# Places in SBUF of the weight buffers and split operands moved by 16-byte steps; a spare strip dropped

## The chip, the cores and the metric

The kernel runs on one core of one Trainium2 chip, in one launch. The metric is the device time of a run in microseconds (us), of which the median of three runs is given. Beside it stands one execution taken by the hardware profiler, and from that one come all the rows below.

## What is computed

Hash-bucketed attention over q, k, v (2 batches, 8 heads, 768 positions, head width 64), then a dense feed-forward layer, then four experts that are mixed by probabilities:

```python
mask = q_bucket[:, :, :, None] == k_bucket[:, :, None, :]
scores = np.where(mask, scale * np.matmul(q, k.transpose(0, 1, 3, 2)), -1e9)
x = softmax(scores) @ v                     # -> 1536 x 512
h = x @ w_in                                # 512 -> 2048
x = np.where(h > 0, h, exp(min(h, 0)) - 1) @ w_out
p = domain_probs / domain_probs.sum(-1)
for e in range(4):                          # 512 -> 1024 -> 512
    out += p[:, e:e + 1] * (np.maximum(x @ w1[e], 0) @ w2[e])
```

All of it is float32. The kernel writes an operand x as a rounded high part and a rest (`hi` + `lo`, both of type fp32r), and makes one product of three matmuls: hi by hi, hi by lo, lo by hi.

## The kernel before

**Stages.** The attention comes first (to about 260 us of the span). Its end is woven into the first layer (`l1_mm`, `emit_l2`), which goes on to about 533 us. What the change's words call the second part, the experts, fills the rest (`second`, `unit`).

**The first layer** goes over (group g, block tb of 512 tokens, tile m of 128 hidden units). `l1_parts` (lines 714 to 716) makes 12 matmuls: the stationary operand is a piece of the weight tile `wt[g, m]`, the moving operand 512 columns of `xh` or `xl`. `emit_l2` (line 768) makes 12 more per tile, with pieces of the same weight tile stationary and 512 columns of the split activations `h` moving.

**The second part** goes over eight half experts gg and three token blocks tb, 24 units in all. In a unit `a_step` computes the next unit's hidden rows in four goes of 12 matmuls (lines 968 to 970: stationary a piece of a split `w1` tile, moving 512 columns of `xh`, `xl`, `xh`). Between them stand seven `product` calls (line 1021, 12 matmuls each). There the stationary operand is 128 columns of a split operand `op`, and the moving operand 256 columns of a split `w2` tile. The products come as 24, 24, 24 and 12 matmuls in a row. The order is written out by hand in `unit`; no scheduler changes it.

**Each matmul has its own weight load** (LDWEIGHTS, the page's PEld), and the load of a matmul runs while the matmul before it streams its moving operand.

**Buffers.** A split weight tile is `[P, 4, DM]`, 8192 bytes of each partition: for the first layer w_in hi, w_in lo, w_out hi, w_out lo. Eight slots are used in turn (`GM = 8`): two in pool `wa`, one in `wm`, five in `wb` (`wpool`). `split_w` takes a slot for the first layer, `slot_tile` one for the second part (two slots for `w1` and four for `w2` in each half expert). The split operands take turns in four halves of two `far` buffers of 8192 bytes (`prep_op`, `op_n % 4`). They are written by ScalarE (hi) and VectorE or GpSimd (lo), in `split2` (lines 906, 908, 910).

**Where tiles lie.** Pools grow from the left end of a partition's memory (`const`, `xp`, `wa`, `raw`, `cv`, `wb`, `near`, `accp`, ...) or from its right end (`edge`, `raw2`, `raw3`, `wm`, `far`, ...). A pool's tile begins at a multiple of 32 bytes. Two tiles only set where the others lie: `pn` is given 64 columns though 48 are used, and `edge_t` is a strip of 96 bytes at the right end, of which `emit_probs` uses 48 as scratch. With them every operand of a matmul begins at a multiple of 64 bytes.

Of the kernel before, what the change touches and what calls it, by code (L numbers as in the profile page):

```python
# [7 lines left out]
F32 = mybir.dt.float32  # L8
F32R = mybir.dt.float32r
# [7 lines left out]
P = 128  # L17
# [18 lines left out]
def lsh_attention_moe_kernel(  # L36
# [15 lines left out]
    B, H, S, D = q.shape  # L52
    NB = proj.shape[1]
    NT, DM = out.shape
    DFF = w_in.shape[1]
    E = dprobs.shape[1]
    NJ = S // P
# [6 lines left out]
    TB = 512  # L64
# [17 lines left out]
    const = ctx.enter_context(tc.tile_pool(name="const", bufs=1))  # L82
# [2 lines left out]
    wa_p = ctx.enter_context(tc.tile_pool(name="wa", bufs=NPRE))  # L85
    raw_p = ctx.enter_context(tc.tile_pool(name="raw", bufs=1))
    cv_p = ctx.enter_context(tc.tile_pool(name="cv", bufs=1))
    edge = ctx.enter_context(tc.tile_pool(name="edge", bufs=1, side="right"))
    edge_t = edge.tile([P, 24], F32, name="edge")


    late, slots, early, ps_early, ps_late = (ExitStack() for _ in range(5))
# [75 lines left out]
    def x_tiles(c):  # L168
        if c not in xh:
            xh[c], xl[c] = (xp.tile([P, NT], F32R, tag=f"x{n}{c}", name=f"x{n}{c}") for n in "hl")  # L170
        return xh[c], xl[c]

    for c in range(NC - 1):
        x_tiles(c)
    pn = const.tile([P, 64], F32, name="pn")[:, 0:B * NJ * E].rearrange("p (t e) -> p t e", e=E)

    def emit_probs():
        sm = edge_t[:, 0:B * NJ]
        nc.vector.tensor_add(sm, dp[:, :, 0], dp[:, :, 1])
        for e in range(2, E):  # L180
            nc.vector.tensor_add(sm, sm, dp[:, :, e])
        nc.vector.tensor_scalar(out=sm, in0=sm, scalar1=1e-9, scalar2=None, op0=ALU.add)
        nc.vector.reciprocal(out=sm, in_=sm)
        nc.vector.tensor_tensor(out=pn, in0=dp, in1=sm.unsqueeze(2).to_broadcast([P, B * NJ, E]),
                                op=ALU.mult)
# [5 lines left out]
    wraw, w32, wt = {}, {}, {}  # L191
# [72 lines left out]

    def split_w(g, m, pool, eng, part=None):
        if part != 1:
            wt[g, m] = pool.tile([P, 4, DM], F32R, tag="w", name="w")
        t = wt[g, m]
        for i, s in enumerate(w32[g, m]):
            if part == 1 - i:  # L270
                continue
            hi, lo = t[:, 2 * i, :], t[:, 2 * i + 1, :]
            if i == 0:
                hi = hi.rearrange("p (c f) -> p c f", f=P)
                lo = lo.rearrange("p (c f) -> p c f", f=P)
            if "p" in eng:
                nc.gpsimd.tensor_scalar(out=hi, in0=s, scalar1=1.0, scalar2=1.0, op0=ALU.mult, op1=ALU.mult)
            else:
                nc.scalar.activation(out=hi, in_=s, func=ACTF.Copy)
            if "P" in eng:  # L280
                nc.gpsimd.tensor_tensor(out=lo, in0=s, in1=hi.bitcast(F32), op=ALU.subtract)
            else:
                nc.vector.tensor_tensor(out=lo, in0=s, in1=hi.bitcast(F32), op=ALU.subtract)
        if part != 0:
            del w32[g, m]
# [356 lines left out]
    def att_step(u):  # L642
# [36 lines left out]
        if g2 >= 1 and m <= NPRE and u < NU:  # L679
            if i == 0 and k_ == 0:  # L680
                pre[:] = conv_w(0, m, cv_p, 2) + [lambda: consumed(0, m, False)]
                pre.extend(lambda n=n: split_w(0, m, wpool(m), "pP", n) for n in range(2))
                pre.append(lambda: consumed(0, m, True))
            for _ in range(i in PRE_AT if m < NPRE else LASTN[i]):
                if pre:
                    pre.pop(0)()


    pools, acc, last_x = {}, {}, []
# [36 lines left out]
    def four(pool, i, dtype, name):  # L726
        return pools[pool].tile([P, 4, TB], dtype, tag=f"{pool}{i}", name=name)
# [53 lines left out]
    def epilogue(g, tb, i, ps):  # L781
# [6 lines left out]
        if g == G1 - 1:  # L788
            last_x.append(lambda: split2(xh[i][:, ts], xl[i][:, ts], a, "av"))
            if tb < NTB - 1:  # L790
                last_x.pop()()

    def wpool(m):
        return wa_p if m < NPRE else pools["wb" if m > NPRE else "wm"]

# [27 lines left out]
    def new_conv():  # L823

        due, (g, m) = todo.pop(0)
        steps = conv_w(g, m, pools["w32"], 2)
        conv.extend((0, f) for f in steps[:6])
        conv.extend(ends)
        conv.extend((0, f) for f in steps[6:] + [lambda: consumed(g, m, False)])
        ends[:] = [(due, lambda i=i: split_w(g, m, wpool(FT.index((g, m)) % GM), "a", i)) for i in range(2)]  # L830
        ends.append((due, lambda: consumed(g, m, True)))
        if not todo:
            conv.extend(ends)
# [31 lines left out]
    ch_n, op_n, op_b = [0], [0], []  # L865

    def slot_tile():
        k_ = slot_n[0] % GM
        slot_n[0] += 1
        return wpool(k_).tile([P, 4, DM], F32R, tag="w", name="w")  # L870

    def emit_pt():

# [29 lines left out]
    def split2(hi, lo, x, eng):  # L903

        if eng[0] == "a":
            nc.scalar.activation(out=hi, in_=x, func=ACTF.Copy)  # L906
        else:
            nc.vector.tensor_copy(hi, x)
        e = nc.gpsimd if eng[1] == "p" else nc.vector
        e.tensor_tensor(out=lo, in0=x, in1=hi.bitcast(F32), op=ALU.subtract)  # L910

    def prep_w1(gg, i):

        t = slot_tile()
        x, _ = raw2(gg, i)
        for j in range(2):
            w1_t[gg, 2 * i + j] = t[:, 2 * j], t[:, 2 * j + 1]
            hi, lo = (y.rearrange("p (c f) -> p c f", f=P) for y in w1_t[gg, 2 * i + j])
            split2(hi, lo, x[:, :, j * P:(j + 1) * P], "av")
# [3 lines left out]
    def prep_w2(gg, n):  # L923

        t = slot_tile()
        b1, b2 = raw2(gg, 0)[1], raw2(gg, 1)[1]
        b11, b12, b21, b22 = b1[:, :, 0:HD], b1[:, :, HD:DM], b2[:, :, 0:HD], b2[:, :, HD:DM]
        tmp = keep["tmp"]
        v = lambda out, a, b_: nc.vector.tensor_tensor(out=out, in0=a, in1=b_, op=ALU.subtract)
        for j, nm in enumerate(PAIRS[n]):  # L930
            hi, lo = (t[:, 2 * j + k_].rearrange("p (k d) -> p k d", k=2) for k_ in range(2))
            if nm == "T2":
                v(b11, b12, b11)
                v(tmp, b22, b11)
            if nm == "T3":
                v(b12, b22, b12)
            if nm == "T4":
                v(b21, b21, tmp)
            x = {"B11": b11, "B21": b21, "T2": tmp, "T3": b12, "T1": b11, "T4": b21, "B22": b22}[nm]
            split2(hi, lo, x, "ap" if n in (1, 2) else "av")  # L940
            t_t[gg, nm] = hi, lo
        if n == 3:
            for _ in range(2):
                raw_free.append(raw_used.pop(0))
            loads()
# [32 lines left out]
    def blocks(u):  # L978
        h = hf_t[u]
        return h[:, 0:2, 0:HT], h[:, 2:4, 0:HT], h[:, 0:2, HT:TB], h[:, 2:4, HT:TB]  # L980

    def prep_op(u, nm, eng="av"):
        a11, a12, a21, a22 = blocks(u)
        x = {"P1": a11, "P2": a12, "P3": a12, "P4": a22, "P5": keep.get("S1"), "P6": keep.get("S2"), "P7": a21}[nm]
        i = op_n[0] % 4
        op_n[0] += 1
        if i % 2 == 0 and len(op_b) < 2:
            op_b.append(four("far", i // 2, F32R, "op"))
        hi, lo = (op_b[i // 2][:, i % 2 * 2 + k_] for k_ in range(2))
        op_t[u, nm] = hi, lo  # L990
        hi, lo = (y.rearrange("p (k t) -> p k t", k=2) for y in (hi, lo))
        split2(hi, lo, x, eng)
# [55 lines left out]
    def unit(v, a, hooks):  # L1048
# [6 lines left out]

        rows(0)
        prep_op(v, "P7")
        product(v, "P1")
        nc.scalar.activation(out=keep["s1"], in_=pr_t["P1"], func=ACTF.Copy)
        product(v, "P2")  # L1060
        sums_op(v, "S4")
        prep_op(v, "P5")
        add_ps(v, "11", "P2", "s1")
        add_kept(v, "11", "s1")
        store(v, "11")
        hooks[0]()
        rows(1)
        prep_op(v, "P4")
        product(v, "P6")
        nc.vector.tensor_tensor(out=keep["u2"], in0=pr_t["P6"], in1=keep["s1"], op=ALU.add)  # L1070
# [110 lines left out]
    for u in range(NU - 2):  # L1181
        att_step(u)
        if u == PU - 2:
            emit_probs()
        if u == NU - PU - 1:
            early.close()
            for i in range(2):
                raw_free.append(open_pool(f"raw{i + 2}", 1, "right"))
            open_pool("wm", 1, "right")
            loads()  # L1190
        if u == NU - PU + 6:
            l1_start(0)
        take(parts, 1)
# [52 lines left out]
```

## Time and profile before

| | before |
|---|---|
| median of 3 runs | 1032.09 us (1031.25 to 1032.11) |
| the profiled execution: its own time | 1030.52 us |
| the profiled execution: its span | 1028.7 us |
| TensorE busy | 1008.8 us, 98% of the span |
| VectorE busy | 841.9 us, 82% |
| ScalarE busy, GpSimd busy | 521.4 us, 494.9 us |
| TensorE clock granted | full in all 40 slices |

Busy time of TensorE says that a matmul was somewhere in the array, not that the array took a column in each cycle: matmuls overlap, and their ends are modelled. So the pace is read from starts: from the start of one row of matmuls to the start of the next, over their number.

### The profile page before, as it was taken

Reading aid. Unit: us, or ns where it says so; the run is one execution under the profiler, and the core shown is the slowest. Engines: PE = TensorE matmul, PEld = TensorE weight load, DVE = VectorE, ACT = ScalarE, POOL = GpSimd, SP = SyncE. Lnnn points to the kernel's source line nnn. Section 1 sums busy time; section 2 is a strip of 40 time slices with the busy share of each in tenths; the row PEclk is TensorE's granted clock in tenths of the full one; section 3 lists DMA queues with packets and bytes.
Section 4 is the critical chain, followed back from the end, with each engine's and each line's share of the span. In section 5 each row is a group of like instructions: output and inputs, shape, how many; then the busy total and the mean of one; then the engine's idle time right before and its main releaser. Section 6 shows DMA issues by size and latency. Waiting matters only on the chain.

```text
span 1028.7 us, 16096 instructions
## 1 busy us (share of the span) xinstructions
PE 1008.8 (98%) x5886; PEld 886.5 (86%) x5886; DVE 841.9 (82%) x1292; ACT 521.4 (51%) x1024; POOL 494.9 (48%) x425
## 2 busy tenths in 40 slices
PE   8999999999999999999999999999999999999997
PEld 5898999888887888888789999999999999999996
DVE  6889888988779898624557778899899999989996
ACT  6898899898566445434523333333243233333332
POOL 3566676575356445522321243545545444454453
PEclk9999999999999999999999999999999999999999
DMA  6856566471122222100020030020200102010012
GB/s 160 186 137 161 129 168 154 111 213 58 41 83 84 81 82 82 42 1 22 5 88 1 1 103 12 1 82 8 96 11 18 65 11 93 11 49 34 1 52 72
DMA packets 72693, 72.23 MB, mean 70 GB/s; under 512 B 26132, under 2 KB 60648, under 8 KB 72616
## 3 DMA queue, kind: packets, MB, share of 16 engines
q1 hardware_dynamic: 72312, 71.14, 24.5%
q8 instruction: 47, 0.77, 0.3%
q14 instruction: 30, 0.25, 0.1%
q10 hardware_dynamic: 304, 0.07, 0.1%
HBM read 48.98 MB, written 3.21 MB: 51 GB/s over the span
## 4 chain that ended last, share of the span: by engine, by line
PE 49%; issue 6%; POOL 2%; DVE 1%; ACT 0%; DVEq 0%; POOLq 0%; ACTq 0%
PE l L1021 22%; PE r L969 4%; PE a L969 4%; PE a L968 4%; PE r L968 4%; PE r L970 4%; PE a L970 4%; POOL h L752 2%; PE l L768 1%; DVE op L910 0%; DVE a L1038 0%; DVE a L1032 0%; ACT op L906 0%; PE r L716 0%; PE r L714 0%
## 5 line engine op out<-in xcount | busy, mean ns | idle before, releaser
L1021 PEld LDWEIGHTS l<-w,op 128*128 128x128 f32 x2016 | 251.0, 188 | 8.5 <-ACT op L906 1.1
L1021 PE MATMUL l<-w,op 128*128 128x256 f32 x2016 | 253.5, 280 | 0.8 <-ACT op L906 0.6
L1038 POOL TENSOR_TENSOR a<-a,temps 128x512 f32<-128x512 f32 x62 | 94.9, 1531 | 127.1 <-DVE a L1032 127.1
L906 ACT ACTIVATE op<-hf 128x512 fp32r<-128x512 f32 x120 | 73.8, 626 | 137.3 <-DVE hf L973 84.4
L768 PE MATMUL l<-h,w 128*128 128x512 f32 x576 | 140.5, 392 | 1.1 <-ACT a L785 0.8
L910 DVE TENSOR_TENSOR op<-hf,op 128x512 fp32r<-128x512 f32 x120 | 126.8, 1070 | 5.1 <-ACT op L906 5.0
L752 POOL TENSOR_TENSOR h<-g,h 128x512 fp32r<-128x512 f32 x44 | 66.4, 1509 | 134.1 <-ACT h L748 89.1
L768 PEld LDWEIGHTS l<-h,w 128*128 128x128 f32 x576 | 107.4, 188 | 26.6 <-POOL h L752 2.2
L395 DVE TENSOR_SCALAR_CACHE_REDUCE mk<-s 128x768 f32<-128x768 f32 x96 | 91.3, 951 | 21.1 <-PE s L386 18.1
L428 DVE TENSOR_TENSOR ptl<-pt,pth 128x384 fp32r<-128x384 f32 x192 | 97.6, 550 | 11.1 <-ACT pth L431 11.1
L414 PE MATMUL pt<-cst,mk 128*128 128x128 f32 x576 | 94.9, 274 | 0.6 <-DMA rx<-d 0.4
L404 ACT ACTIVATE mk<-mk,mn 128x768 f32<-128x768 f32 x96 | 89.7, 935 | 10.8 <-DVE mk L395 10.2
L431 ACT ACTIVATE pth<-pt 128x384 fp32r<-128x384 f32 x192 | 84.0, 482 | 8.1 <-PE pt L414 7.7
L385 PE MATMUL s<-ks,qs 128*128 128x512 f32 x192 | 80.3, 441 | 7.6 <-DVE mk L395 7.2
L414 PEld LDWEIGHTS pt<-cst,mk 128*128 128x128 f32 x576 | 71.1, 140 | 12.7 <-ACT mk L404 5.4
L969 PE MATMUL a<-xl,w 128*128 128x512 f32 x192 | 75.1, 391 | 0.0
L969 PE MATMUL r<-xl,w 128*128 128x512 f32 x192 | 75.0, 391 | 0.0
L968 PE MATMUL a<-xh,w 128*128 128x512 f32 x192 | 75.0, 391 | 0.0
L968 PE MATMUL r<-xh,w 128*128 128x512 f32 x192 | 75.0, 390 | 0.0
L970 PE MATMUL r<-xh,w 128*128 128x512 f32 x192 | 74.7, 389 | 0.0
L970 PE MATMUL a<-xh,w 128*128 128x512 f32 x192 | 74.7, 389 | 0.0
L444 PE MATMUL pv<-pth,vs 128*128 128x384 f32 x192 | 72.1, 376 | 0.0
(158 smaller groups left out, 2138.6 us busy)
## 6 DMA issues: line engine op xcount, KB each, us to landing
raw<-in_moe_w_dram SPq DMA_DIRECT2D x32, 512.0 KB
raw<-in_moe_w_in_dram SPq DMA_DIRECT2D x16, 512.0 KB
raw<-in_moe_w_out_dram SPq DMA_DIRECT2D x16, 512.0 KB
ks<-kh SPq DMA_DIRECT2D x15, 384.0 KB
qs<-qh SPq DMA_DIRECT2D x30, 192.0 KB
sk<-in_k_dram SPq DMA_DIRECT2D x8, 384.0 KB
sq<-in_q_dram SPq DMA_DIRECT2D x8, 384.0 KB
ks<-kl SPq DMA_DIRECT2D x16, 192.0 KB
```

Source lines behind the costliest of these rows:

```text
L395: nc.vector.tensor_scalar(out=e_t[u], in0=s_t.pop(u)[:, 0:S], scalar1=MASKED, scalar2=None, op0=ALU.min, op1=ALU.min, accum_out=mn)
L404: nc.scalar.activation(out=e, in_=e, func=ACTF.Exp, bias=mn_t.pop(u), scale=-1.0, accum_out=sums_t[g2][:, j, par:par + 1])
L414: nc.tensor.transpose(pt[:, i * P:(i + 1) * P], e_t[u][:, kb * P:(kb + 1) * P], ident)
L428: nc.vector.tensor_tensor(out=lo, in0=pt, in1=hi.bitcast(F32), op=ALU.subtract)
L752: eng.tensor_tensor(out=hl[:, cs], in0=gt[:, cs], in1=hh[:, cs].bitcast(F32), op=ALU.subtract)
L768: mm(ps, a, b_, start=(m == 0 and n == 0), stop=(m == GS[g] - 1 and n == 2))
L910: e.tensor_tensor(out=lo, in0=x, in1=hi.bitcast(F32), op=ALU.subtract)
L968: mm(ps, wh[:, cs], xh[c][:, ts], start=(c == 0), stop=False)
L969: mm(ps, wh[:, cs], xl[c][:, ts], start=False, stop=False)
L970: mm(ps, wl[:, cs], xh[c][:, ts], start=False, stop=(c == NC - 1))
L1021: mm(ps[:, tt * HD:(tt + 1) * HD], a[:, cs], b_[:, k_], start=(n == 0), stop=(n == 11))
L1038: e.tensor_tensor(out=x, in0=x, in1=keep[nm], op=ALU.add)
```

## The change

Three things change, all of them places in memory.

1. `pn` is made with the columns that it uses, and the scratch of `emit_probs` becomes a `const` tile, `psum_e`. The strip `edge` is gone, so all pools at the right end move up by 96 bytes, less what item 3 takes.
2. A slot of pool `wb` grows from 8192 to 8224 bytes, and the weights begin 0 or 16 bytes into it, by `(0, 4, 0, 4, 4)` elements in turn. The slots in `wa` and `wm` stay as they are.
3. An operand buffer in `far` grows to 8224 bytes as well, and its second half begins 16 bytes later than before.

The order of the instructions and their sizes are the same on every engine. One VectorE and one GpSimd instruction of the weight conversion in the first layer have further waits on transfers, since their tile now overlaps other old tiles.

The places in the two built programs, as the start address modulo 64 bytes:

| operand | before | after |
|---|---|---|
| `xh`, `xl` | 0 | 0 |
| weight slots: `wa`, `wa`, `wm` | 0, 0, 0 | 0, 0, 32 |
| weight slots: the five of `wb` | 0, 0, 0, 0, 0 | 0, 48, 0, 48, 16 |
| `op`, four halves | 0, 0, 0, 0 | 32, 48, 0, 16 |
| `h` in `near`; in `far` | 0; 0 | 32; 32 and 0 |

Modulo 128 bytes, before: 64 for `xh`, `xl`, `wa`, `wb` and `near`, and 0 for `wm`, `far` and `op`.

```diff
-    edge = ctx.enter_context(tc.tile_pool(name="edge", bufs=1, side="right"))
-    edge_t = edge.tile([P, 24], F32, name="edge")
...
-    pn = const.tile([P, 64], F32, name="pn")[:, 0:B * NJ * E].rearrange("p (t e) -> p t e", e=E)
+    pn = const.tile([P, B * NJ, E], F32, name="pn")
...
-        sm = edge_t[:, 0:B * NJ]
+        sm = const.tile([P, B * NJ], F32, name="psum_e")
...
-            wt[g, m] = pool.tile([P, 4, DM], F32R, tag="w", name="w")
+            wt[g, m] = w_tile(pool)
...
+    w_n = [-1]
+
+    def w_tile(pool):
+        if pool is not pools.get("wb"):
+            return pool.tile([P, 4, DM], F32R, tag="w", name="w")
+        w_n[0] += 1
+        o = (0, 4, 0, 4, 4)[w_n[0] % 5]
+        t = pool.tile([P, 4 * DM + 8], F32R, tag="w", name="w")
+        return t[:, o:o + 4 * DM].rearrange("p (i d) -> p i d", i=4)
...
-        return wpool(k_).tile([P, 4, DM], F32R, tag="w", name="w")
+        return w_tile(wpool(k_))
...
-            op_b.append(four("far", i // 2, F32R, "op"))
-        hi, lo = (op_b[i // 2][:, i % 2 * 2 + k_] for k_ in range(2))
+            op_b.append(pools["far"].tile([P, 4 * TB + 8], F32R, tag=f"far{i // 2}", name="op"))
+        o = i % 2 * (2 * TB + 4)
+        hi, lo = (op_b[i // 2][:, o + k_ * TB:o + (k_ + 1) * TB] for k_ in range(2))
```

## Rows read from the trace of the kernel before

**Rows 1.** The page: span, busy time by engine, and slices of the span.
```profile
span 1028.7 us, 16096 instructions
PE 1008.8 (98%) x5886; PEld 886.5 (86%) x5886; DVE 841.9 (82%) x1292; ACT 521.4 (51%) x1024; POOL 494.9 (48%) x425
...
PEclk9999999999999999999999999999999999999999
```

**Rows 2.** Busy time by stretch (from:to in us): its length, then each engine.
```profile
420.00:470.00 50.00, 50.00 (x222) 41.36 (x221) 16.90 (x26) 18.67 (x30) 16.12 (x11) 1.00 0.00 1
...
700.00:800.00 100.00, 100.00 (x638) 90.83 (x637) 92.05 (x115) 34.66 (x62) 50.23 (x36) 1.00 0.13 40
800.00:900.00 100.00, 100.00 (x634) 90.70 (x633) 93.19 (x115) 33.45 (x60) 48.99 (x34) 1.00 0.12 40
```

**Rows 3.** Waits of TensorE, 420 us to the end: total us, times, longest.
```profile
PE l L1021 <- ACT op L906: 0.6, 1, 0.6
```

**Rows 4.** The chain that ended last, in the second part: start us, us, what.
```profile
539.42 2.82 PE l L1021 x24
542.25 0.23 PE a L968
...
544.98 2.82 PE l L1021 x24
547.80 0.23 PE r L968
...
550.53 1.41 PE l L1021 x12
...
554.67 2.87 PE l L1021 x24
```

**Rows 5.** The page's costliest groups: matmuls by line, count, busy us, mean ns.
```profile
L1021 PE MATMUL l<-w,op 128*128 128x256 f32 x2016 | 253.5, 280 | 0.8 <-ACT op L906 0.6
...
L768 PE MATMUL l<-h,w 128*128 128x512 f32 x576 | 140.5, 392 | 1.1 <-ACT a L785 0.8
...
L968 PE MATMUL a<-xh,w 128*128 128x512 f32 x192 | 75.0, 391 | 0.0
```

**Rows 6.** TensorE in the first layer by start (modelled length behind it), two places.
```profile
262.97 8.60 PE L768 MATMUL l<-h,w 128*128 128x512 f32 x36
271.41 0.39 PE L714 MATMUL a<-xh,w 128*128 128x512 f32 x1
...
431.60 0.39 PE L714 MATMUL r<-xh,w 128*128 128x512 f32 x1
...
434.32 2.88 PE L768 MATMUL l<-h,w 128*128 128x512 f32 x12
437.04 0.39 PE L714 MATMUL a<-xh,w 128*128 128x512 f32 x1
```

## The prediction

> **What bounds the kernel now.** I read the page first, then the stretches, the waits, and last the chain for the pace. The page has TensorE at 98% of the span with its clock granted in full throughout [rows 1], so there is no gap to close and no clock to win back. By stretches TensorE is busy for 100.00 of 100 us in the second part and for 50.00 of 50 in the first layer, while VectorE stands at 92 to 93 in the second part and at 17 of 50 in the first layer [rows 2]. From 420 us on TensorE waited for others once, for 0.6 us [rows 3]. So from there to the end the time is a count of matmuls by their pace, and an edit there pays or costs by what it does to the pace of a single matmul, as long as VectorE can follow.
>
> The pace comes from starts. Two products take 2.82 us for 24 matmuls of 256 columns, 117.5 ns each; one takes 1.41 us for 12, the same [rows 4]. A set of 12 with 512 columns takes from 431.60 to 434.32, and the next 12 to 437.04: 2.72 us, 226.7 ns each [rows 6]. The 256 columns by which they differ take 226.7 - 117.5 = 109.2 ns. So of the 117.5 ns of a short matmul 109.2 are its columns, and 117.5 - 109.2 = **8.3 ns stay over** that no column explains. Something at each matmul costs them, and the weight load of the next one, which runs under it, is the candidate.
>
> That places in memory count for this shows in two pairs of rows. A pair of products takes 2.87 us instead of 2.82 at 554.67 [rows 4]; its `w2` tile lies in slot `wm`, at 0 modulo 128 bytes as `op` does, where other slots lie at 64. That is 0.05 us over 24, 2.1 ns each. And the first 36 matmuls of line 768, whose `h` lies in `far`, take from 262.97 to 271.41: 8.44 us, at most 234.4 ns each (a wait at the head would be in it), against 226.7 later, so up to 7.7 ns each [rows 6]. Same instruction, same sizes, other places.
>
> **The change part by part.** No instruction is added, removed or moved: 2016 matmuls of line 1021, 576 of line 768 and 192 in each of the groups of lines 968 to 970 stay what they are [rows 5].
>
> The strip and `pn`: five small VectorE instructions write elsewhere, during the attention. Nothing. The further waits of two weight-conversion instructions are for transfers of the attention's operands that landed long before; behind them stand other conversions on VectorE and GpSimd, with VectorE busy for 16.90 of 50 us in the first layer [rows 2]. Nothing; without that cover it would be one wait of a transfer, not one for each matmul.
>
> Larger slots and offsets: what they change is the distance between the operand that a matmul streams and the one that is loaded under it for the next. Before, this distance is a multiple of 64 bytes at every matmul. By the addresses of the changed program it is so no longer at 1426 of the 2016 of line 1021, 730 of the 1152 of lines 968 to 970, 359 of the 576 of lines 714 to 716 and 429 of the 576 of line 768: 2944 matmuls. All lie where TensorE has no slack, so each ns counts in full.
>
> What one of them gains or loses, no row shows, because no operand before is off a multiple of 64 bytes. The bounds: it can't gain more than what stays over, 8.3 ns, so 2944 x 8.3 = 24.4 us at most. On the other side the dearest placing in the rows costs 2.1 ns for a short matmul and 7.7 for a long one: 1426 x 2.1 + 1518 x 7.7 = 3.0 + 11.7 = 14.7 us more. Between them I take a gain of the size that one step of place is shown to have, 2.1 ns [rows 4]: the same line with everything else equal, and the dear one there is the one whose two operands lie alike, modulo 128 bytes. That is 2944 x 2.1 = **6.2 us**.
>
> VectorE: if TensorE takes 24.4 us less, some 18 of them in the second part's 488 us, VectorE's 92 to 93 of 100 us become 96 [rows 2]. It still fits, with little left, and some of the largest gain may go into waits. At the forecast's gain it is no bound. VectorE, ScalarE and GpSimd write to the offset places as well; their instructions are some 0.5 us and more long and a start that is 16 bytes off should be lost in that, which no row shows.
>
> What speaks against: the Trainium skill (TensorE: Matmul & The Clock Gate, part 2, on what happens when you issue a matmul) says that TensorE has two independent read ports and that "Loading the next tile's weights doesn't steal SBUF read bandwidth from the running matmul". By it there would be nothing to gain, and the sum would be 0. The trace agrees in that the loads don't add their whole length, and differs in the 2.87 against 2.82 us.
>
> **The rivals.** *Most of the rest goes* (the forecast's mechanism at its bound). For: 8.3 ns is over at every matmul, also where the distance is 64 modulo 128, which suggests that steps of 64 bytes don't part the two reads and smaller ones might. Against: nothing shows a matmul without it. Time: 1030.52 - 24.4 = 1006.1 us in the profiled execution, 1008 by the median.
>
> *Nothing.* The rest is the price of changing weights, whatever the places, or dear and cheap distances balance, since 4320 - 2944 = 1376 of the matmuls keep a multiple of 64. Against: the two pairs of rows. Time: 1032 us.
>
> *Slower: the new distances are dearer than the old ones.* [...] For: places have shown to cost up to 7.7 ns where they are bad, which is more than the 2.1 ns that a good one was seen to give, and the kernel's two spare tiles put every operand on a multiple of 64. Against: the dear rows lie at multiples of 64 as well. Price: if half of the 2944 take the dearest price, 7.3 us, so 1037.9 us in the profiled execution and 1039.5 by the median; all of them, 1045.2 and 1047. It decides as soon as the mean over the new distances is over today's 117.5 and 226.7 ns.
>
> *The change doesn't do what it says*: the addresses of the built program have moved as described, so no chance is given to this.
>
> **How the numbers follow.** The profiled execution took 1030.52 us, 1.6 below the median of 1032.09, and 1.8 more than its span. Forecast: 1030.52 - 6.2 = 1024.3, by the median 1025.9, so 1026 us. Chances: the forecast, a gain of 2 to 13 us, 0.34; most of the rest goes, over 13 us, 0.20; nothing, 0.17; slower, 0.29. About 0.2% (2 us) is what a measurement of this kernel can tell from no change. So faster 0.54, same 0.17, slower 0.29. The range reaches from just under the whole rest (1008) to just over half of the matmuls at the dearest price (1039.5): 1006 to 1041. Some 0.08 may lie above it and 0.05 below.
>
> **What would show it.** Right: the chain's 24 matmuls take less than 2.82 us, by 0.05 us or more at those products whose distance isn't a multiple of 64, and the sets of 12 with 512 columns less than 2.72; products that keep the distance stay at 2.82 to 2.87. If nothing matters, both stay everywhere. If the slower rival is right, rows with 2.9 us and over for 24, or 2.8 and over for 12, stand where the places are off. Wrong in another way: matmuls get faster and waits of TensorE for VectorE or ScalarE appear at line 1021 in place of the 0.6 us; or VectorE's 92 us of 100 grow though its instructions are the same.

## The result, and the profile after

| | before | after |
|---|---|---|
| median of 4 runs each | 1031.67 us | 1040.26 us (1039.8 to 1041.3) |
| ratio | | 1.0089 [1.0076, 1.0103] |
| span of the profiled execution | 1028.7 us | 1038.0 us |

The changed kernel is slower by 8.6 us, 0.9%. The page of after, its span and busy times (of before: [rows 1]):

```profile
span 1038.0 us, 16098 instructions
...
PE 1019.0 (98%) x5886; PEld 890.4 (86%) x5886; DVE 838.6 (81%) x1292; ACT 522.3 (50%) x1024; POOL 495.7 (48%) x425
```

The counts of matmuls and of VectorE, ScalarE and GpSimd instructions are those of before. TensorE is busy for 10.2 us more, and the other engines for what they were, within 3.3 us. The same stretches as [rows 2], in after (from:to, length, busy time of PE, PEld, DVE, ACT, POOL, then clock, DMA share, GB/s):

```profile
700.00:800.00 100.00, 100.00 (x630) 90.19 (x629) 90.88 (x114) 33.97 (x61) 50.46 (x35) 1.00 0.10 30
800.00:900.00 100.00, 100.00 (x628) 90.16 (x627) 91.05 (x112) 33.00 (x60) 50.62 (x36) 1.00 0.16 51
```

TensorE is still busy for all of 100 us at a full clock, but takes 630 and 628 matmuls in them where it took 638 and 634. VectorE has a little less to do in the same time: 91 us of 100, not 92 to 93. TensorE's waits from 420 us to the end (for, total us, times, longest) are the single one of [rows 3], under its new line numbers:

```profile
PE l L1030 <- ACT op L914: 0.6, 1, 0.6
```

So each matmul takes longer. The chain in the second part of after (start us, us, what; between two of these rows stand the 12 long matmuls of a step, whose time is the gap):

```profile
538.73 2.77 PE l L1030 x24
...
643.79 2.86 PE l L1030 x24
...
649.43 2.86 PE l L1030 x24
...
655.10 2.82 PE l L1030 x24
...
660.73 1.43 PE l L1030 x12
...
664.95 2.84 PE l L1030 x24
```

The short products, 2.82 us for 24 in [rows 4], have spread to both sides: 2.77 in the first row, 2.86 in the next two. The long sets that are shown have only grown. From 643.79 + 2.86 = 646.65 to 649.43 a set of 12 takes 2.78 us; the next two take 655.10 - 652.29 = 2.81 and 660.73 - 657.92 = 2.81, the fourth 664.95 - 662.16 = 2.79. By the addresses these four stream at 112, 160, 160 and 112 bytes from what is loaded, modulo 256; the sets of [rows 4] at 0. In [rows 4] they take 2.73 (542.25 to 544.98, 547.80 to 550.53). In the first layer it is the same (TensorE by start, the modelled length behind it):

```profile
429.52 0.39 PE L712 MATMUL r<-xh,w 128*128 128x512 f32 x1
...
432.31 2.97 PE L766 MATMUL l<-h,w 128*128 128x512 f32 x12
435.12 0.39 PE L712 MATMUL r<-xh,w 128*128 128x512 f32 x1
```

The 12 matmuls from 429.52 take 2.79 us, the 12 from 432.31 take 2.81, against 2.72 in [rows 6].

Taking the time from the start of each matmul to the start of the next, and adding up by line, gives where the 9.3 us of the span went:

| matmuls | before, us | after, us | difference |
|---|---|---|---|
| products, 256 columns (L1021, now L1030), 2015 steps | 239.2 | 239.9 | +0.7 |
| steps of the second part, 512 columns (L968 to 970, now L976 to 978), 1152 | 262.6 | 266.5 | +3.9 |
| first layer, first half (L714 to 716, now L712 to 714), 576 | 132.1 | 133.6 | +1.5 |
| first layer, second half (L768, now L766), 576 | 133.3 | 135.5 | +2.2 |
| all others (attention above all) | 253.4 | 254.5 | +1.1 |

The last line lies between 253.2 and 255.0 us in the profiles of all kernels below but one, also where nothing of the attention's operands moved, so it is put down to no edit. (TensorE's clock may have a part in it: in the profile of after it was granted at 0.50, 1.2 GHz, from 15 to 20 us, and in that of before at 1.00.) The two rows of the first layer are to be read together, since a wait of about 1 us lies in its first half in before and in its second half in after and in all kernels below. The first four make +8.2 us: the long matmuls pay 7.6 of them, the short ones 0.7.

### The profile page after: what moved, and what is told of

Its sections match the earlier page's. It is cut to its first block, busy times and chain, and to the rows that moved or that the text cites. A ratio compares the mean times of both kernels' runs of the same rounds, so it can differ in the third digit from the quotient of the medians.

```text
span 1038.0 us, 16098 instructions
## 1 busy us (share of the span) xinstructions
PE 1019.0 (98%) x5886; PEld 890.4 (86%) x5886; DVE 838.6 (81%) x1292; ACT 522.3 (50%) x1024; POOL 495.7 (48%) x425
## 4 chain that ended last, share of the span: by engine, by line
PE 78%; DVE 8%; issue 7%; ACT 2%; POOL 2%; DMA 1%; DVEq 0%; SPq 0%; POOLq 0%; ACTq 0%
PE l L1030 22%; PE l L766 8%; PE a L976 4%; PE a L977 4%; PE a L978 4%; PE r L976 4%; PE r L978 4%; PE r L977 4%; PE pt L412 4%; PE s L383 3%; PE pv L442 2%; PE pv L443 2%; POOL h L750 2%; DVE ptl L426 2%; PE s L384 2%
## 5 line engine op out<-in xcount | busy, mean ns | idle before, releaser
L1030 PEld LDWEIGHTS l<-w,op 128*128 128x128 f32 x2016 | 251.5, 188 | 9.2 <-ACT op L914 1.1
L1030 PE MATMUL l<-w,op 128*128 128x256 f32 x2016 | 254.2, 281 | 0.8 <-ACT op L914 0.6
L766 PE MATMUL l<-h,w 128*128 128x512 f32 x576 | 141.8, 395 | 1.2 <-POOL h L750 1.1
L766 PEld LDWEIGHTS l<-h,w 128*128 128x128 f32 x576 | 107.7, 188 | 27.5 <-POOL h L750 2.6
L918 DVE TENSOR_TENSOR op<-hf,op 128x512 fp32r<-128x512 f32 x120 | 121.2, 1021 | 5.1 <-ACT op L914 4.9
L976 PE MATMUL a<-xh,w 128*128 128x512 f32 x192 | 75.6, 394 | 0.0
L976 PE MATMUL r<-xh,w 128*128 128x512 f32 x192 | 75.5, 393 | 0.0
```

The costliest lines, as they stand in the source:

```text
L766: mm(ps, a, b_, start=(m == 0 and n == 0), stop=(m == GS[g] - 1 and n == 2))
L976: mm(ps, wh[:, cs], xh[c][:, ts], start=(c == 0), stop=False)
L1030: mm(ps[:, tt * HD:(tt + 1) * HD], a[:, cs], b_[:, k_], start=(n == 0), stop=(n == 11))
```

## The experiments

**The theory** after the result, called D in the texts below: the pace of a matmul follows from the *distance*, the start address of the operand that it streams less that of the operand being loaded under it. The expectations count it modulo 128 bytes at first and modulo 256 from `pitch128` and `far192` on; below it is given modulo 256 where nothing else is said. The rival: an operand that starts off a 64-byte border costs, whatever the distance. A second rival: one part of the change carries the whole loss.

**The parts alone.** `strip_alone` has only the strip and `pn` of the change; it moves all of the right end, and with it `op`, `wm`, `far`, so that 1660 short matmuls go from a distance of 64 to 224. `w_alone` has only the `wb` slots. `strip_op` has the strip and the operand buffers (without the room of the strip the larger buffers don't fit in the memory).

```diff
# strip_alone: these lines of the change, and no others
-    edge_t = edge.tile([P, 24], F32, name="edge")
...
-    pn = const.tile([P, 64], F32, name="pn")[:, 0:B * NJ * E].rearrange("p (t e) -> p t e", e=E)
+    pn = const.tile([P, B * NJ, E], F32, name="pn")
...
-        sm = edge_t[:, 0:B * NJ]
+        sm = const.tile([P, B * NJ], F32, name="psum_e")
# w_alone: w_tile and its two calls, and no others
...
+        o = (0, 4, 0, 4, 4)[w_n[0] % 5]
+        t = pool.tile([P, 4 * DM + 8], F32R, tag="w", name="w")
# strip_op: strip_alone and
+        o = i % 2 * (2 * TB + 4)
```

> The strip and pn as in the change, weight slots and operand buffers as before: the pools at the right end move by 96 bytes, so op lies 96 bytes off a multiple of 128, wm too. Theory D (the pace of a matmul is set by the distance, modulo 128 bytes, of the operand that it streams from the one loaded under it; read from the changed kernel: short matmuls about 119.7 ns at 0 and 96, 117.8 at 64, 116.7 at 32, 118.5 to 119 at the others; long ones 226.7 at 0 and 229 to 234 elsewhere): 1660 short ones go from 64 to 96, +3.3 us, and 216 long ones from 64 to 96, +0.9: about 1036 us. Theory B (an operand that begins off a 64-byte border costs more, whatever the distance): op and wm now lie 32 off a border, all 2016 short ones pay 1 to 2 ns: 1034 to 1036. Rival O (only the weight offsets matter): 1032.

> The weight slots of wb as in the change, strip and operand buffers as before. Theory D: long matmuls as in the changed kernel, +6.7 us, short ones over all distances, +1.0: about 1039.5 us, so nearly the whole of the change. Theory B: weights off a border in three of eight slots, 1036 to 1040. If the operands' offsets were the cause: 1032 to 1034.

> The strip and the operand buffers as in the change, weight slots as before. Theory D: short matmuls at distances 0, 16, 32, 48, 64 and 112 in place of 64, +1.3 us, long ones with wm +1.1: about 1034.5 us. Theory B: three of four halves of op off a border: 1034 to 1036.

Measured: `strip_alone` 1035.87 us, ratio 1.0051 [1.0034, 1.0067]; `w_alone` 1037.98, 1.0072 [1.0057, 1.0087]; `strip_op` 1033.67, 1.0027 [1.0017, 1.0037]; before 1030.58. All three are slower. They don't add up: 5.3 and 7.4 us alone against 8.6 for the whole, and `strip_op` costs less than the strip that it contains. That fits a pace that hangs on the distance between two operands, since moving both can undo it, and not a price of a place by itself. The second rival is not quite out: the weight slots alone make 7.4 of the 8.6 us, and their interval overlaps that of the whole. But they aren't the only part that costs, since the strip alone costs 5.3. That `strip_alone` came out at the 1036 us expected is luck in part: the theory had 3.3 us of it on short matmuls and 0.9 on long ones, and by the starts the short ones cost 0.8 and the long ones of the second part 3.2. The chain of `strip_alone`, as above:

```profile
703.17 2.83 PE l L1019 x24
...
708.79 2.84 PE l L1019 x24
...
714.37 2.84 PE l L1019 x24
```

Here the products moved by 0.01 to 0.02 us. The set behind the first (706.00 to 708.79, distance 224) takes 2.79 us, the one behind the second (711.63 to 714.37, distance 0) 2.74. Same kernel, same line, 4 ns a matmul apart.

**Is it the distance, or the border?** `lock32` puts the operands of the products 32 bytes off a 64-byte border, with distances chosen by the theory: nearly all long matmuls at 0 modulo 128, as most of before, and most short ones at 64 modulo 128. The `w1` tiles lie at their slot's start (`slot_tile(0)`), the `w2` tiles 8 elements into it.

```diff
-    edge_t = edge.tile([P, 24], F32, name="edge")
...
+        n = 8 if pool is pools["wm"] else 32
+        t = pool.tile([P, 4 * DM + n], F32R, tag="w", name="w")
+        return t[:, o:o + 4 * DM].rearrange("p (i d) -> p i d", i=4), o > 0
...
-        t = slot_tile()
+        t, _ = slot_tile(0)
...
-        t = slot_tile()
+        t, _ = slot_tile(8)
...
+        o = i % 2 * 2 * TB + (8 if i < 2 else 0)
```

> Places chosen by theory D: all eight weight slots at the distance 0 for the long matmuls (wm too, which was at 64), and w2 put 32 bytes further in its slot (in wm and wb) and op 32 as well, so that the short ones keep the distance 64 (1444 of them; 547 stand at 32) though both operands lie 32 off a 64-byte border. Theory D: no slower than before; 1444 short ones either stay at 117.8 ns or take the faster pace of 113.3 ns that the changed kernel shows at this distance where a product follows long matmuls: 1023 us if they do, 1030 if not. Theory B: w2 and op off a border in 1512 of the 2016 short ones: 1034 or more.

Measured: 1031.98 us, 1.0016 [1.0003, 1.0029]. That is neither the 1023 or 1030 us of the theory nor the 1034 or more of the border. The sum hides two effects. Its chain, and its first layer by start:

```profile
703.04 2.72 PE l L1027 x24
...
708.55 2.74 PE l L1027 x24
...
734.76 2.72 PE l L1027 x24
```

```profile
424.88 2.89 PE L766 MATMUL l<-h,w 128*128 128x512 f32 x12
427.61 0.39 PE L712 MATMUL r<-xh,w 128*128 128x512 f32 x1
...
430.33 2.96 PE L766 MATMUL l<-h,w 128*128 128x512 f32 x12
433.12 0.39 PE L712 MATMUL r<-xh,w 128*128 128x512 f32 x1
```

The products fell to 2.72 us for 24, 113.3 ns each, with operands off the border: for them the border costs nothing, and 4.5 of the 117.8 ns can go. The products gave back 5.0 us in all. But of the long sets every other one is dear: 424.88 to 427.61 is 2.73 us, 430.33 to 433.12 is 2.79. By the addresses the first set stands at 0, the second at 128 modulo 256. The long ones lost 3.8 (second part), 2.6 and 0.1 us (first layer). So for them 128 is not like 0.

**Modulo 128 or 256?** `pitch128` makes the slots of `wb` 128 bytes longer and leaves all else: every address keeps its place modulo 128. `far192` moves the left end by -64 and the right end by +64 bytes, so that short matmuls go from 64 to 192 and long ones keep their distance, bar those of `wm` and a few with `h` in `far`. In `far192`, and in `wm0`, `lock256`, `lock256e0` and `all32` below, the last VectorE instruction of `emit_probs` becomes four as well, since the scratch lies in `pn`.

```diff
# pitch128
+        n = 32 if pool is pools.get("wb") else 0
+        t = pool.tile([P, 4 * DM + n], F32R, tag="w", name="w")
# far192
-    edge_t = edge.tile([P, 24], F32, name="edge")
+    edge.tile([P, 8], F32, name="edge")
...
-    pn = const.tile([P, 64], F32, name="pn")[:, 0:B * NJ * E].rearrange("p (t e) -> p t e", e=E)
+    pn = const.tile([P, B * NJ, E], F32, name="pn")
...
-        sm = edge_t[:, 0:B * NJ]
+        sm = pn[:, :, 0]
...
+        for e in range(E - 1, -1, -1):
+            nc.vector.tensor_tensor(out=pn[:, :, e], in0=dp[:, :, e], in1=sm, op=ALU.mult)
```

> Only the slots of wb grow, by 128 bytes, with nothing put off in them: every operand keeps its place modulo 128 bytes, but two of the eight slots, near and what follows move by 128 modulo 256. Theory D256: 288 + 144 long matmuls with w and 337 with h go from 0 to 128, about +5 ns each, and 418 short ones from 64 to 192, about 3 ns off: +3 us, 1034 us. If the distance counts modulo 128, or only 64-byte borders count: no change, 1031.

> All operands on multiples of 64 bytes as before the change, but the left end of the memory 64 bytes lower (pn trimmed, the scratch of emit_probs inside pn) and the right end 64 higher: the short matmuls go from the distance 64 to 192 modulo 256 (1660 of 2016), the long ones stay at 0, except those with wm (64 to 192). Theory D256 (the distance counts modulo 256 bytes: long 226.7 ns at 0, 229 at 16 to 80, 232 to 234 at 128 to 240; short 120 at 0 and 128, 117.8 or 113.3 at 64, mostly 113.3 at 192; read from the runs so far): 1660 short ones 3 to 4.5 ns less, 270 long ones 4 ns more: 4 to 6.5 us off, about 1026 us. If only the distance modulo 128 counts: no change, 1031. Theory B (64-byte borders) expects no change either, 1031.

Measured: `pitch128` 1035.64 us, 1.0043 [1.0028, 1.0059]: the period is not 128 for the long ones (+1.5, +0.5 and +2.4 us on the three lines of the table), so the expectation by 256 held. `far192` 1034.75, 1.0052 [1.0037, 1.0067], a miss: the products did not go to the cheap pace that 192 had seemed to bring in `lock32`. Its chain:

```profile
713.87 2.83 PE l L1019 x24
...
719.44 2.83 PE l L1019 x24
```

139 of its 144 products at 192 ran at 118 ns. The four groups of matmuls lost 2.1 us by their starts; the other 2.3 us of its difference are not explained. Its profile can't tell, since it is of the slowest of its six runs (1039.35 us). There the attention took 6.6 us more, and TensorE's clock stood at half, 1.2 GHz, for 6.8 and for 3.4 us in it. One stretch of `far192`, then of before (the clock is the third number from the end, 35 matmuls stand against 62):

```profile
20.00:30.00 10.00, 7.36 (x35) 6.10 (x34) 5.06 (x12) 5.92 (x14) 5.98 (x8) 0.76 0.93 246
20.00:30.00 10.00, 9.25 (x62) 8.03 (x61) 8.18 (x19) 8.64 (x20) 7.49 (x10) 1.00 0.92 244
```

`pitch128` shows both paces at the same distance, a few microseconds apart:

```profile
701.73 1.36 PE l L1026 x12
...
705.84 2.72 PE l L1026 x24
...
711.30 2.83 PE l L1026 x24
...
716.89 2.82 PE l L1026 x24
```

The first two rows stand at 64 and take 113.3 ns, the last one stands at 64 as well and takes 117.5. So distance alone doesn't set the pace of a short one. In `lock32` and in after the cheap pace had come where the last long matmul led into the product at 16 or 32, and in `pitch128` at some of the products behind long sets at 128 or 64; in before, where it leads in at 64 out of a settled set, it never came.

**Is it the start of the row?** `lock256` (n is 64 for four slots of `wb`, 24 for `wm`, 0 for the others; the `w2` tiles lie 8 elements into their slots) holds all long matmuls at 0 modulo 256 and 1239 short ones at 64, 742 at 32, with 32 at the step from the long matmuls into the product (the offset of `w2` is taken where the slot has room for it). `lock256e0` has the long ones and the 64 alike, but goes from the long ones into the product at 0. `wm0` has the places of before, with the odd slot `wm` brought to 0 (long) and 64 (short) like the rest.

```diff
# lock256
+        t = pool.tile([P, 4 * DM + n], F32R, tag=tag, name="w")
...
+        t = slot_tile(8)
...
+            op_b.append(pools["far"].tile([P, 4 * TB + 8 * (i // 2)], F32R, tag=f"far{i // 2}", name="op"))
# lock256e0, against lock256
-        t = slot_tile(8)
+        t = slot_tile(16)
...
-            op_b.append(pools["far"].tile([P, 4 * TB + 8 * (i // 2)], F32R, tag=f"far{i // 2}", name="op"))
+            op_b.append(pools["far"].tile([P, 4 * TB], F32R, tag=f"far{i // 2}", name="op"))
# wm0, against before
+        n = 24 if pool is pools.get("wm") else 0
...
+            op_b.append(pools["far"].tile([P, 4 * TB + 16 * (i // 2)], F32R, tag=f"far{i // 2}", name="op"))
```

> As lock32, but every long matmul stands at the distance 0 modulo 256 bytes and not only modulo 128 (slots of wb 8448 bytes apart, near moved with them, wm at 0 too). The short ones: 1239 at 64, 742 at 32. If lock32 lost on its long matmuls what it won on its short ones because half of them stood at 128, that loss goes: short ones 4 to 5 us less than before as there, long ones with h and of the first layer as before or 0.6 us better, long ones between the products up to 2.4 us more since a product in the faster pace leaves them a slower start: about 1027 to 1028 us. If the distance counts modulo 128 alone, lock256 equals lock32: 1031 to 1032.

> As lock256, but w2 lies 64 bytes further in its slot and op not at all: 1296 short matmuls at 64 again, 719 at 0, and the load of the first op of a product stands at 0 from the x that is streamed then, not at 32. If the start decides which of the two paces at 64 a product takes, the 113.3 ns of lock256 may give way to 117.8: 1031 us if so, 1027 if the 113.3 ns stay.

> Back to the places of before, with one mend: slot wm is brought to the distance 0 for the long matmuls, as the other seven slots are (and so to 64 for the short ones). Theory D with long distances counted modulo 256 bytes: 288 short matmuls 120 to 117.8 ns, 288 long ones 229 to 226.7: -1.3 us, about 1029 us beside 1030.4 of before. Rival (places only have to be multiples of 64): no change.

Measured: `wm0` 1031.31 us, 1.0007 [0.9995, 1.002], no difference that can be told, where 1.3 us less was expected; by the starts its four groups took 1.3 us less. `lock256e0` 1034.02, 1.0038 [1.0026, 1.0051], 3 us over what was expected: all products at 64 run at 117.8 ns (one of the 108 holds a wait). `lock256` 1031.06, 0.9999 [0.999, 1.0008], where 1027 to 1028 was expected: 98 of 108 products at 64 run at 113.3. So the way in goes with the pace that a product at 64 gets, and nearly always keeps. The two kernels differ in one more thing, since in `lock256e0` every operand lies on a multiple of 64 bytes. The border doesn't decide by itself, though: in `lock32` 66 products at 64 run at 113 and 23 at 118, all off the border, and in `pitch128` 12 and 96, all on it. The chains, `lock256` first, then `lock256e0`:

```profile
539.80 2.88 PE l L1032 x24
...
545.48 2.73 PE l L1032 x24
...
550.99 1.36 PE l L1032 x12
...
555.14 2.73 PE l L1032 x24
```

```profile
722.47 2.83 PE l L1032 x24
...
728.06 2.83 PE l L1032 x24
```

In `lock256` the products take 2.73 us (the first row holds two single steps of 165 and 222 ns), 5.1 us less in all, and the first layer's pace is back: its profile has 2.72 us for the set from 429.41,

```profile
429.41 2.88 PE L764 MATMUL l<-h,w 128*128 128x512 f32 x12
432.13 0.39 PE L710 MATMUL r<-xh,w 128*128 128x512 f32 x1
```

which settles 256 against 128 for the first layer, where nothing else was changed for the long ones. The time alone would have fitted the 1031 to 1032 us of a period of 128. A longer period doesn't show: settled long matmuls at 0 and at 256 modulo 512 take 227.0 and 227.1 ns. Yet the time shows no gain. The gaps in the chain show where most of it went: the set behind the second product goes from 548.21 to 550.99, 2.78 us, the one behind the third from 552.35 to 555.14, 2.79, where [rows 4] have 2.73, although the distance is 0 in both. The starts show what happens in these 12 steps (ns, the set behind the chain's 548.2 in `lock256`, then the one behind 542.25 in before):

```
234 240 229 233 236 224 231 236 228 233 231 235
233 231 226 227 227 226 227 227 226 227 227 225
```

A set at distance 0 settles to 226.7 ns over a fixed sequence of steps, 240 229 234 236 224 231 236 228 233 231 227 (give or take two, with a first step that may lie outside it), and where in it the set begins goes with how the matmuls ahead of it ended. Behind a product at 113.3 it begins near the front and the set is over before it has settled. 54 of 96 sets of the second part came behind such a product and took 232.5 ns a step; in all, the long matmuls of the second part lost 3.6 us of the 5.1 that the products had won.

**A version from what was learned.** `all32` puts the `w2` tiles at the slot's start: 1924 short matmuls at 32, whose 116.6 ns showed in `lock256` with a milder sequence behind it.

```diff
# against lock256
-        t = slot_tile(8)
+        t = slot_tile(0)
```

> As lock256, but the w2 slots begin at the slot's start, so that 1924 of 2016 short matmuls stand at distance 32 and none at 64; the long ones stay at 0 modulo 256 (bar 92 that lead into a product). By the paces that lock256 showed: products at 32 run 116.6 ns against 117.8 at 64 in the kernel before, 1924 x 1.2 = 2.3 us less, up to 4 with the starts; the 96 sets of 12 long matmuls behind a product at 32 ran 229.6 there against about 227.4 in the kernel before, 96 x 12 x 2.2 = 2.5 us more. Distance theory with what is given back: within 2 us of the kernel before, ratio 0.997 to 1.001. If the long matmuls behind aren't touched: 3 to 4 us faster, ratio 0.996 to 0.997. If the order at the start decides otherwise for 32 (products at 118 to 120): slower by 2 us or more.

Measured: 1030.83 us, 1.0008 [0.9999, 1.0017], as the distance theory with the give-back had it. Its chain:

```profile
545.07 2.80 PE l L1032 x24
...
550.62 1.40 PE l L1032 x12
...
554.77 2.80 PE l L1032 x24
```

2.80 us for 24 instead of 2.82; by the starts the products won 2.6 us, and the 96 long sets of the second part ran at 229.4 ns a step, and lost 1.7. No version beat before.

**The paces put together.** From the starts of all twelve profiles, in stretches of 11 matmuls or more at one distance, the mean of the last steps, rounded (the distance modulo 256, from the addresses of the built programs; a commoner pace stands first):

| distance | 512 columns, ns | 256 columns, ns |
|---|---|---|
| 0 | 227 (228 to 231 while it settles) | 120 |
| 16 | 228 | 117, 120 |
| 32 | one stretch: 233 | 117; seldom 118 to 120 |
| 48 | none | 117 |
| 64 | 229 | 118 or 113 |
| 80, 96 | 229 (80) | 119 to 120 |
| 112 | 233 to 234, or 227 | 113 (12 of 22 stretches), 119 to 120 |
| 128 | 233 | 120 |
| 144 to 176 | 234 to 235 (160), 232 (176) | 117 to 119 |
| 192 | 233 | 118 or 113 |
| 208 to 240 | 233 (208, 224) | 117 to 119 |

For 512 columns 0 is the cheapest place and everything from 128 on is dear; before, 1923 of the 2304 long matmuls stood at 0. The border rival fails for them too: in `pitch128` every operand lies on a multiple of 64, and it is 5.3 us slower than before. In the profiles the four groups' sum differs from before's by +8.2 (after), +4.4 (`strip_alone`), +7.0 (`w_alone`), +2.4 (`strip_op`), +1.6 (`lock32`), +2.1 (`far192`), +3.9 (`pitch128`), +2.4 (`lock256e0`), -1.3 (`wm0`), -1.7 (`lock256`) and -1.1 us (`all32`). The timed differences follow these within 2.3 us, mostly from above: a profile's gain of 1 to 2 us, as in the last three, did not show in the times. The granted clock has a part in that. Over the 152 runs in which it is on record, a run whose mean clock is 0.001 lower took about 0.6 us longer than another run of the same kernel (an estimate, from a straight line through their times and clocks). The runs of `lock256` had a mean clock of 0.9956 and those of before beside them 0.9973, which is worth about 1 us; so at the same clock `lock256` would be nearly 1 us faster than before, and `wm0` and `all32` no faster. What lowered the clock isn't shown.

## Why the prediction went wrong

The time lay in the range, by the slower rival; the forecast had the wrong sign.

- **What bounds the kernel** was right. TensorE is busy in every microsecond of the second part, before and after, with one wait of 0.6 us; no instruction moved; VectorE did not become a bound, since TensorE got slower. Strip and `pn` show no cost as instructions: `wm0` has no strip either, and its time can't be told from that of before. As places they do: `strip_alone` costs 5.3 us.
- **The pace from starts** (117.5 and 226.7 ns) was right, and it is how the loss was found. The 8.3 ns that "no column explains" were not: the subtraction takes the rest to be the same for both shapes, and with the 113.3 ns that the runs found it would leave 113.3 - 113.4, nothing. What the runs show is that 4.5 ns of a short matmul can go by placing alone, and that no long one ran steadily under 226.
- **The bounds**, 24.4 us less to 14.7 us more, held: the 2944 matmuls took about 7.6 us more.
- **The failed step** is "Between them I take a gain of the size that one step of place is shown to have, 2.1 ns". It gave -6.2 us; the four groups measured +8.2. Two things were wrong in it. The sign came from one pair of rows of the 256-column line, where the dear place is the one at distance 0; it was carried over to the 1518 long matmuls, for which 0 is the cheapest place. And it counted every leave from a multiple of 64 as a way out of a bad place, while most of the long ones, 1229 of the 1518, stood at 0 before and had nothing to gain. By the starts (steps that hold a wait left out), the 1518 long ones took 7.0 us more, 4.6 ns each, and the 1426 short ones 0.6 us, 0.4 ns each. The 786 other long ones, put at nothing, took 1.5 us more: some moved to other multiples of 64, and some stand behind matmuls whose pace had changed. The second pair of rows, up to 7.7 ns dearer for `h` in `far`, spoke of the long ones: 24 of those 36 stand at 192, dear in the table, and 12 at 0, still settling. It was used for the bound alone.
- **The slower rival** had the mechanism in its first half ("the new distances are dearer than the old ones") and the price: half of the 2944 at the dearest, +7.3 us and 1039.5, against 1040.26. That the half was about right is luck, since no row spoke for it, and the border of 64 bytes is not the reason (`lock32`, `lock256`). Of its signs in the trace, 2.8 us and over for 12 came (2.81); 2.9 and over for 24 came hardly at all, since most dear rows show 2.83 to 2.87.
- **Most of the rest goes, by places alone**: about half of it goes for short matmuls (4.5 of 8.3 ns), in kernels built for it, and the long ones behind them give most of that back.
- The sentence of the Trainium skill (TensorE: Matmul & The Clock Gate, part 2) that the weight load doesn't steal read bandwidth from the running matmul would have made the sum 0. The runs don't show who takes what from whom; they show that the pace of a long matmul moves by some 7 ns with the distance of the two operands, so the sum was not 0.

What stays open: why the distance acts, why with 256, and why the way in picks the pace of a short one. Within a set the stationary operand in use and the next one lie at the same place modulo 256, so these runs can't tell which of the two the streamed operand meets. That the weight load is the cause was argued, not shown; a row of matmuls that keeps its weights was not tried.

## What to carry to other kernels

Where TensorE is the bound, read its pace from starts, for each shape by itself, and list the address distance of streamed and loaded operand modulo 256 for each group of matmuls before moving a buffer: a strip of 96 bytes at an end of the memory cost 0.5% here (`strip_alone`). A sign that is read from one shape is not carried to another: look first which group has anything to gain. A gain in one row of matmuls is to be counted with the row behind it.

## What was not expected of the hardware

- The pace of fp32r matmuls with a weight load each depends on the distance of their operands: 226.7 ns at 0 against 232 to 235 from 128 to 224 for 512 columns, 113.3 to 120 for 256.
- The same product at the same distance of 64 has two steady paces, 117.8 and 113.3 ns, and nearly always keeps the one that it begins with (98 of 108 at 113.3 in `lock256`, none in `lock256e0`).
- A change of distance is followed by up to ten steps off the pace, in a sequence that repeats from run to run to the nanosecond or two; what it costs depends on where in it the row begins.
